# An attention and two dense layers on one core: the start addresses of the tiles in SBUF are shifted

## The chip, the cores and the metric

The kernel runs on one core of a Trainium2 chip. The metric is the time of one execution on the device in microseconds (us). The kernel before was timed three times: 1668.88, 1672.46 and 1673.58 us, median 1672.46. Everything read from a trace below belongs to one further, profiled execution.

## The reference

Three stages follow each other. All inputs and results are float32.

```python
# attention: q, k, v are (8, 8, 576, 64); p is (8, 8, 32, 64)
p_packed = softmax(p @ k.T / 8) @ v
x = softmax(q @ p_packed.T / 8) @ p_packed          # -> (4608, 512)
# layer 1: w_in (512, 2048), w_out (2048, 512); a has 4 numbers, b has 2
h = x @ w_in
g = (a0 + a1*h + a2*h**2 + a3*h**3) / (1 + |b0|*|h| + |b1|*h**2 + 1e-6)
x = g @ w_out
# layer 2: w2_in (512, 2048), w2_out (2048, 512), alpha (2048,)
h = x @ w2_in
out = (max(h, 0) + alpha * min(h, 0)) @ w2_out
```

The weights come as 64-bit numbers, are rebuilt as float32 on the chip, and each float32 operand of a large matmul is split into a high and a low part of type fp32r. A product is then three matmuls (high by high, high by low, low by high).

## The kernel before, in words

**Stages.** The attention stage runs from 0 to about 221 us. It works in 16 steps (8 batches, two groups of four heads), with plain float32 matmuls of 256 or 288 columns (L237, L250, L265, L289), and writes its result to DRAM. In the same time the weights of layer 1 are loaded and split, and `emit_Wb` (L334) multiplies `w_in` by the packed values of the attention (`pph`, which lies in `spw` on the right for even pairs of batches, the first pair's until 111 us among them, and in `gp` on the left for odd ones), so that layer 1 works on 256 instead of 512 inputs. Layer 1 follows, from about 221 to 870 us, and layer 2, from 870 us to the end.

**Layer 1.** The tokens come in 9 chunks of 512, the 2048 inner columns in 8 parts, which makes 72 steps `g`. A step has `emit_L1` (L470: first product into `h`; a chunk crosses a batch border, so its matmuls are 64 to 512 columns wide), `emit_E1` and `emit_E2` (the rational function on DVE, ACT and POOL) and, three steps later, `emit_L2` (L541: 24 matmuls of 512 columns). Beside this DVE, ACT and POOL rebuild the weights of layer 2 (`w2_step`; L568 to L598). Two PSUM buffers hold `h`, so that L470 of a step waits until E2 of two steps earlier is done.

**Layer 2.** 9 chunks by 16 inner parts make 144 steps. Each has 12 matmuls of `emit_L3` (L660), the activation (`emit_prelu`), and 12 matmuls of `emit_L4` (L741). All are 512 columns wide, and each has its own weight load of 128 columns.

**Which operand streams.** A matmul loads one operand of 128 columns as weights, and the other, the moving operand, streams through the array. The moving operands are `a2t` (L470), `gt` (L541), `yt` (L660) and the `w2_out` tiles `wo` (L741); the weights are `wb`, `wo`, `wb` and `vt`.

**Order.** The program is in written order on each engine (`manual_schedule`, L46): the loops at L383 to L391 for the attention, the letters of `ORDER` and `DRAIN` for the order inside, the loops at L684 and L754 for the layers.

**Layout of SBUF.** [...] Pools on the left side are stacked upwards from the bottom, pools on the right side downwards from the top, and a tile takes a multiple of 32 bytes. At the bottom lie the scratch of 1024 bytes (L801), four framework constants (128 bytes), then `const` with `ident` (512), `coef` (32), `alpha_sb` (64), `babs` (32) and `qc` (32): 1824 bytes, which is 3 x 512 + 288. Every later tile that the layers use on the left (`wp`, `gp`, then `spa` or `spb`) is a multiple of 512 bytes long, so all of them start at 288 bytes past a multiple of 512. On the right 32 bytes are in use at the very top, and the tiles of `spx` (`a2t`) and of `spy0`, `spy1` (`yt`) start at 480 bytes past a multiple of 512. The slices that a matmul reads are multiples of 512 bytes from there, with the exception of `a2t`, where a piece may begin at an odd multiple of 256 bytes. From the sizes follows also that the third `gt` buffer covers bytes 196384 to 204575 of a partition, and `yt` of the odd chunks (`spy1`) bytes 196576 to 212959.

The pool `sp0` (L163) holds the tiles of the attention alone; its space is used again by `spa` (L457) and `spb`. `ident` is the unit matrix by which TensorE transposes (L250, L251, L276).

Of the kernel before, what the change touches and what calls it, by code (L numbers as in the profile page):

```python
# [10 lines left out]
F32 = mybir.dt.float32  # L11
# [15 lines left out]
def attention_then_two_moes(ctx, tc, qT, kT, v, pT, w_in, w_out, ab, w2_in, w2_out, alpha, out):  # L27
    nc = tc.nc
# [18 lines left out]
    const = ctx.enter_context(tc.tile_pool(name="const", bufs=1))  # L47
# [1 line left out]
    gp = ctx.enter_context(tc.tile_pool(name="gp", bufs=1))  # L49
    dr = ctx.enter_context(tc.tile_pool(name="dr", bufs=1, space=DRAM))  # L50

    ident = const.tile([128, 128], F32, name="ident")
    make_identity(nc, ident)
    coef = const.tile([128, 6], F32, name="coef")
    nc.sync.dma_start(out=coef, in_=ab)
    alpha_sb = const.tile([128, NF], F32, name="alpha_sb")
# [2 lines left out]
    act(babs, coef[:, 4:6], AF.Abs)  # L59
    qc = const.tile([128, 1], F32, name="qc")  # L60
    pool.memset(qc, 1.0 + 1e-6)
    a0, a1c, a2c, a3 = (coef[:, i:i + 1] for i in range(4))
    b0, b1 = babs[:, 0:1], babs[:, 1:2]

# [88 lines left out]
    def open_pool(name, **kw):  # L153
        opened[name] = ExitStack()
        return opened[name].enter_context(tc.tile_pool(name=name, reuse_waits="tile", **kw))
# [7 lines left out]
    sp0 = open_pool("sp0", bufs=2, side="left")  # L163
    ps0 = open_pool("ps0", bufs=1, space=PSUM, side="left")

    mask = sp0.tile([128, 128], F32, tag="mask", name="mask", bufs=1)
    pool.memset(mask, 0.0)
    for h in range(4):
# [640 lines left out]
```

## Time and profile before

| what | value |
|---|---|
| median of three runs | 1672.46 us |
| profiled execution | 1673.79 us |
| span of its trace | 1672.0 us |
| PE busy | 1595.5 us (95%) |
| PEld (weight loads) busy | 1294.1 us (77%) |
| DVE busy | 1089.8 us (65%) |
| ACT busy | 778.4 us (47%) |
| POOL busy | 627.4 us (38%) |
| granted clock of TensorE over the span | 0.984 |

Engines are PE (TensorE's matmuls), PEld (its weight loads), DVE, ACT, POOL, and SP, which issues DMAs. A busy PE is not a PE at its peak: a matmul counts as busy from its start to its modelled end, and consecutive ones overlap. The rate is read from start to start.

### The profile page before, as it was taken

How to read it: one execution, taken by the hardware profiler on the slowest of the kernel's cores; microseconds unless marked ns; L12 is line 12 of the kernel's file. 1: busy time of each engine (PE TensorE's matmuls, PEld its weight loads, DVE VectorE, ACT ScalarE, POOL GpSimd, SP SyncE). 2: the span in 40 equal slices, each digit the busy share in tenths (PEclk: the TensorE clock that was granted, in tenths of full speed). 3: DMA queues.
4: the chain of work that ended last, by engine and by line, in shares of the span. 5: the costliest groups of instructions: out<-in, count | busy, mean ns of one | idle time of the engine just before them, and what ended most of it. 6: DMA issues, size and time to landing. Idle time of an engine off the chain costs nothing.

```text
span 1672.0 us, 19305 instructions
## 1 busy us (share of the span) xinstructions
PE 1595.5 (95%) x7424; PEld 1294.1 (77%) x7424; DVE 1089.8 (65%) x1323; ACT 778.4 (47%) x979; POOL 627.4 (38%) x369
## 2 busy tenths in 40 slices
PE   4878879999999999999999999999999999999999
PEld 2444557888888888888888888888888888888887
DVE  6988877999999999999954344344343434343343
ACT  3444578888889888887851111111111111111111
POOL 3443458777887888866650000000001010000000
PEclk9898999999999999999999999999999999999999
DMA  8889962324224242333561010101010101010000
GB/s 304 266 298 323 293 214 85 130 76 138 102 102 138 89 139 102 108 128 121 186 243 47 0 51 0 51 1 51 0 44 7 44 7 44 7 44 7 9 17 25
DMA packets 86683, 169.03 MB, mean 101 GB/s; under 512 B 8000, under 2 KB 45888, under 8 KB 86592
## 3 DMA queue, kind: packets, MB, share of 16 engines
q1 hardware_dynamic: 81984, 151.03, 26.6%
q10 hardware_dynamic: 4608, 16.78, 2.9%
q8 instruction: 58, 0.95, 0.2%
q14 instruction: 33, 0.27, 0.0%
HBM read 110.64 MB, written 57.15 MB: 100 GB/s over the span
## 4 chain that ended last, share of the span: by engine, by line
PE 76%; DVE 9%; DMA 6%; ACT 5%; issue 2%; POOL 2%; SPq 0%; ACTq 0%; POOLq 0%; DVEq 0%
PE u L660 24%; PE acc L741 24%; PE acc L541 16%; PE h L470 10%; DMA s<-in_w_out 3%; DMA wb_d<-wbs 1%; PE pw L334 1%; DVE s L585 1%; DVE h L526 1%; ACT h L521 1%; DVE s L584 1%; PE pp L265 1%; DMA kt<-in_kT 1%; DMA qt<-in_qT 0%; DVE mag L126 0%
## 5 line engine op out<-in xcount | busy, mean ns | idle before, releaser
L660 PE MATMUL u<-yt,wb 128*128 128x512 f32 x1728 | 425.9, 394 | 0.0
L741 PE MATMUL acc<-wo,vt 128*128 128x512 f32 x1728 | 417.4, 390 | 0.0
L541 PE MATMUL acc<-gt,wo 128*128 128x512 f32 x1728 | 406.1, 391 | 0.9 <-ACT yo L486 0.8
L670 ACT ACTIVATE vt<-m 128x512 fp32r<-128x512 f32 x144 | 91.0, 632 | 634.7 <-DVE m L668 634.7
L660 PEld LDWEIGHTS u<-yt,wb 128*128 128x128 f32 x1728 | 323.3, 187 | 77.8
L741 PEld LDWEIGHTS acc<-wo,vt 128*128 128x128 f32 x1728 | 324.2, 188 | 72.3
L541 PEld LDWEIGHTS acc<-gt,wo 128*128 128x128 f32 x1728 | 321.6, 188 | 66.5 <-ACT yo L486 1.6
L667 DVE TENSOR_SCALAR m<-u,alpha_sb 128x512 f32<-128x512 f32 x144 | 108.0, 750 | 317.1 <-PE u L660 317.1
L650 POOL TENSOR_TENSOR yt<-s,yt 128x512 fp32r<-128x512 f32 x36 | 46.7, 1300 | 646.5 <-ACT yt L649 646.5
L470 PE MATMUL h<-a2t,wb 128*128 128x128 f32 (+7 forms) x1536 | 247.2, 317 | 11.9 <-DVE v__1950 L527 6.8
L470 PEld LDWEIGHTS h<-a2t,wb 128*128 128x128 f32 x1536 | 228.3, 191 | 31.3 <-ACT q__1997 L507 7.2
L671 DVE TENSOR_TENSOR vt<-m,vt 128x512 fp32r<-128x512 f32 x144 | 99.6, 692 | 112.6 <-ACT vt L670 112.6
L668 DVE SCALAR_TENSOR_TENSOR m<-u,m 128x512 f32<-128x512 f32 x144 | 99.6, 692 | 5.0
L427 POOL TENSOR_TENSOR wb<-s,wb 128x512 fp32r<-128x512 f32 x64 | 83.9, 1314 | 37.6 <-ACT wb L426 37.5
L334 PE MATMUL pw<-wb,pph 128*128 128x512 f32 x192 | 63.1, 457 | 18.6 <-ACT wbs L346 17.0
L334 PEld LDWEIGHTS pw<-wb,pph 128*128 128x128 f32 x192 | 36.3, 209 | 44.7 <-ACT wbs L346 27.1
L575 DVE TENSOR_SCALAR s<-s 128x512 f32<-128x512 f32 x32 | 50.5, 1579 | 0.0
L598 POOL TENSOR_TENSOR s<-s 128x512 fp32r<-128x512 f32 x32 | 43.0, 1344 | 18.0 <-ACT s L597 18.0
L237 PE MATMUL ps<-kt,pt 128*64 128x288 f32 x128 | 27.0, 558 | 23.7 <-ACT a L243 8.0
L265 PE MATMUL pp<-vt,a1T 128*128 128x256 f32 (+1 forms) x160 | 45.3, 425 | 3.0 <-DMA vt<-in_v 2.3
L346 ACT ACTIVATE wbs<-pw 128x512 f32<-128x512 f32 x56 | 33.0, 591 | 27.6 <-PE pw L334 13.6
L265 PEld LDWEIGHTS pp<-vt,a1T 128*128 128x128 f32 (+1 forms) x160 | 32.0, 211 | 17.3 <-issue 9.3
(1006 smaller groups left out, 2000.3 us busy)
## 6 DMA issues: line engine op xcount, KB each, us to landing
wb_d<-wbs SPq DMA_DIRECT2D x64, 256.0 KB, 4.8
s<-wb_d SPq DMA_DIRECT2D x64, 256.0 KB, 3.7
w_d<-s SPq DMA_DIRECT2D x32, 512.0 KB, 2.6
kt<-in_kT SPq DMA_DIRECT2D x16, 576.0 KB, 6.2
qt<-in_qT SPq DMA_DIRECT2D x16, 576.0 KB, 6.2
y_d<-yo SPq DMA_DIRECT2D x18, 512.0 KB, 3.6
s<-y_d SPq DMA_DIRECT2D x36, 256.0 KB, 3.5
out<-o SPq DMA_DIRECT2D x36, 256.0 KB, 2.1
```

The costliest lines, as they stand in the source:

```text
L265: mm(pp, at[0:kc, c, :], v_[0:kc, c, :], start=c == 0, stop=c == 4)
L334: mm(pw, pph[bp][:, x, j].rearrange("p a b -> p (a b)"), w[:, y, :], start=k == 0, stop=k == 2)
L427: pool.tensor_tensor(t[:, 1], st, t[:, 0], op=ALU.subtract)
L470: mm(h[:, ft, o:o + m], w[x][:, k, 128 * ft:128 * ft + 128], a2_t[c][:, y, k, o:o + m], start=n == 0, stop=n == 5)
L541: mm(acc[d // 2][:, d % 2, :], w[:, x, 128 * d:128 * d + 128], t[:, y, ft, :], start=f == 0 and (x, y, ft) == (0, 0, 0), stop=f == NP - 1 ...
L575: dve.tensor_scalar(w, w, LOW, HIGH, op0=ALU.max, op1=ALU.min)
L660: mm(us[g], w2i[f][:, 1 - x, k, :], yt[c][:, y, k, :], start=n == 0, stop=n == 11)
L667: dve.tensor_scalar(m, u, 0.0, alpha_sb[:, f:f + 1], op0=ALU.min, op1=ALU.mult)
L668: dve.scalar_tensor_tensor(m, in0=u, scalar=0.0, in1=m, op0=ALU.max, op1=ALU.add)
L670: act(t[:, 0], m, AF.Copy)
L671: dve.tensor_tensor(t[:, 1], m, t[:, 0], op=ALU.subtract)
L741: mm(acc2[s], t[:, x, 128 * s:128 * s + 128], w2o[f][:, 1 - y, :], start=f == 0 and n == 0, stop=f == NF - 1 and n == 2)
```

## The change

`ident` moves from the pool `const` to the pool `sp0`, and is built there just before `mask`. Two tiles that nothing reads or writes are added: `fill_left` of 224 bytes at the end of `const`, and `fill_right` of 480 bytes at the top of the right side. With that `const` ends at 1536 bytes (3 x 512), the right side begins at 228864 bytes (447 x 512), and every tile of the two layers, on both sides, starts at a multiple of 512. No instruction is added or removed.

```diff
-    ident = const.tile([128, 128], F32, name="ident")
-    make_identity(nc, ident)
     coef = const.tile([128, 6], F32, name="coef")
...
     qc = const.tile([128, 1], F32, name="qc")
     pool.memset(qc, 1.0 + 1e-6)
+
+    const.tile([128, 56], F32, name="fill_left")
+    top = ctx.enter_context(tc.tile_pool(name="top", bufs=1, side="right"))
+    top.tile([128, 120], F32, name="fill_right")
...
     ps0 = open_pool("ps0", bufs=1, space=PSUM, side="left")
 
+    ident = sp0.tile([128, 128], F32, tag="ident", name="ident", bufs=1)
+    make_identity(nc, ident)
     mask = sp0.tile([128, 128], F32, tag="mask", name="mask", bufs=1)
```

## Rows read from the trace of the kernel before

**Rows 1.** The page's parts 1 and 4: busy us, shares; the chain by engine.
```profile
PE 1595.5 (95%) x7424; PEld 1294.1 (77%) x7424; DVE 1089.8 (65%) x1323; ACT 778.4 (47%) x979; POOL 627.4 (38%) x369
...
PE 76%; DVE 9%; DMA 6%; ACT 5%; issue 2%; POOL 2%; SPq 0%; ACTq 0%; POOLq 0%; DVEq 0%
```

**Rows 2.** Busy time of each engine in four stretches and the end of layer 1; clock and DMA last.
```profile
core 0: us, PE busy (x) PEld busy (x) DVE busy (x) ACT busy (x) POOL busy (x), PEclk, DMA share, GB/s
300.00:453.00 153.00, 153.00 (x818) 135.45 (x818) 144.07 (x123) 133.25 (x141) 119.87 (x62) 1.00 0.32 111
453.00:626.00 173.00, 170.62 (x966) 150.25 (x965) 166.54 (x143) 155.60 (x166) 142.58 (x73) 1.00 0.34 118
626.00:870.00 244.00, 244.00 (x1220) 210.26 (x1220) 216.46 (x186) 200.37 (x206) 172.72 (x86) 1.00 0.40 141
...
848.00:870.00 22.00, 22.00 (x98) 18.20 (x97) 9.39 (x8) 10.67 (x12) 12.27 (x7) 1.00 0.66 247
...
870.00:1672.00 802.00, 798.10 (x3458) 647.59 (x3456) 319.33 (x451) 118.39 (x194) 41.57 (x32) 1.00 0.08 27
```

**Rows 3.** The chain by line in the same four stretches, in that order.
```profile
by line: PE acc L541 60.8%; PE h L470 39.4%
...
by line: issue 13.2%; DVE s L585 6.4%; DVE s L584 5.8%; ACT h L521 5.2%; DVE h L526 4.7%; ACT wb L426 3.1%; DMA s<-wb_d 2.6%; PE h L470 2.3%; ACT s L597 2.2%; ACT a2t L414 1.8%; POOL q__3862 L509 1.4%; POOL q__4488 L509 1.4%; POOL q__3945 L
...
by line: PE acc L541 65.4%; PE h L470 34.7%
...
by line: PE u L660 50.2%; PE acc L741 49.2%; DVE o L747 0.1%; PE acc L541 0.1%; issue 0.0%
```

**Rows 4.** Timeline of PE, one step of layer 2: start, duration to the modelled end.
```profile
1199.96 2.96 PE L660 MATMUL u<-yt,wb 128*128 128x512 f32 x12
1202.76 2.90 PE L741 MATMUL acc<-wo,vt 128*128 128x512 f32 x12
1205.50 0.39 PE L660 MATMUL u<-yt,wb 128*128 128x512 f32 x1
```

**Rows 5.** The chain in layer 1: start, us until the next piece.
```profile
439.05 5.44 PE acc L541 x24
...
812.56 2.80 PE h L470 x12
...
848.62 21.78 PE acc L541 x96
```

**Rows 6.** Matmuls of one line: duration ns minimum/median/maximum, first and last start.
```profile
L660 PE MATMUL u<-yt,wb x1728: 394/394/395, 870.2 to 1656.8; 128*128 128x512 f32 x192
...
L741 PE MATMUL acc<-wo,vt x1728: 388/389/398, 881.4 to 1667.7; 128*128 128x512 f32 x192
...
L541 PE MATMUL acc<-gt,wo x1728: 387/389/501, 245.9 to 870.0; 128*128 128x512 f32 x192
...
L334 PE MATMUL pw<-wb,pph x46: 387/398/796, 66.1 to 111.0; 128*128 128x512 f32 x46
...
L265 PE MATMUL pp<-vt,a1T x6: 377/378/379, 169.4 to 170.5; 128*128 128x256 f32 x6
```

**Rows 7.** Timeline of PE: those six plain float32 matmuls.
```profile
169.45 1.46 PE L265 MATMUL pp<-vt,a1T 128*128 128x256 f32 x6
```

**Rows 8.** Groups of L470 by width: busy us, mean ns, idle before.
```profile
L470 PE MATMUL h<-a2t,wb 128*128 128x512 f32 x192 | 51.6, 421 | 10.2 <-DVE v__1950 L527 6.8 <-DVE v__2067 L527 2.5 <-DVE v__2250 L527 0.9
...
L470 PE MATMUL h<-a2t,wb 128*128 128x256 f32 x192 | 24.0, 281 | 0.9 <-DVE v__4653 L527 0.9
```

**Rows 9.** Timeline of the first microseconds: POOL, and PE's first use of `ident`.
```profile
0.72 0.20 POOL masks.py:197 MEMSET ident<- 128x128 f32 x1 [0.29 <-POOLq L800]
...
1.53 0.70 POOL L170 MEMSET mask<- 32x64 f32 x4
...
4.05 0.85 POOL L179 TENSOR_SCALAR pt<-pt 128x256 f32<-128x256 f32 x1 [1.81 <-DMA pt<-in_pT]
...
18.81 1.11 PE L250 MATMUL pst<-ident,a 128*128 128x128 f32 x4
```

**Rows 10.** Last use of `ident`, and first instruction on `spa`'s space: first and last start.
```profile
L276 PE MATMUL pp<-ident,ppn x16: 270/328/477, 31.7 to 208.1; 128*128 128x128 f32 x16
...
L506 ACT ACTIVATE r__1948<-h x1: 1025/1025/1025, 224.1 to 224.1; 128x1024 f32<-128x1024 f32 x1
```

## The prediction

> **What bounds the kernel now.** I read the page's busy shares first, then its chain, then both by stretch, and last the timeline of single matmuls. PE is busy for 95% of the span and holds 76% of the chain [rows 1]. Layer 2, from 870 us on, is PE alone: L660 and L741 make 99% of its chain, DVE works 319 of 802 us, and the granted clock is 1.00, that is 2.4 GHz [rows 2, 3]. Nothing there waits. So the only thing that can change is how long one matmul occupies the array.
>
> That time is the finding. In a step of layer 2 twelve matmuls of L660 take from 1199.96 to 1202.76, 233.3 ns each, and twelve of L741 until 1205.50, 228.3 ns each [rows 4]. In layer 1, 24 of L541 take 5.44 us, 226.7 ns each, and twelve of L470 at 512 columns take 2.80 us, again 233.3 ns [rows 5]. Widths, clock and weight loads are alike; the rates are not. The two slow lines stream their moving operand from the right side of SBUF (`yt`, `a2t`), the two faster ones from the left (`wo`, `gt`). The modelled durations say it too, by line and with hardly any spread: 394 ns for all 1728 of L660, a median of 389 for L541 and L741 [rows 6].
>
> How far is this from the best that the trace shows? The plain float32 matmuls of the attention, L265, have a duration of 378 ns, and six of them end 1.46 us after the first start, so they start (1460 - 378) / 5 = 216 ns apart [rows 6, 7]. At 2.4 GHz 216 ns are 518 clock periods for 256 columns: two periods a column, and 6 over. A matmul that takes one period a column and pays the same 6 needs 512 + 6, which is 216 ns again. Against that the left side pays 11 ns too much on each matmul and the right side 17.5. The duration is the interval plus 162 ns in all three cases (378 - 216, 389 - 227, 394 - 233), so the excess lies in streaming and not in starting or ending.
>
> Layer 1 has two limits. From 300 to 453 and from 626 to 870 us its chain is L541 and L470 alone; from 453 to 626 it changes among DVE, ACT and POOL [rows 3]. DVE is busy for 144 of 153, 167 of 173 and 216 of 244 us [rows 2].
>
> **Why the address may be the cause.** What separates right from left is either the height in the partition or the start address within some block. Height I can exclude by the layout: the third `gt` buffer and `yt` of the odd chunks share bytes 196576 to 204575, yet no L660 is fast [rows 6], and the last 96 of L541, which pass through all three buffers, take 21.78 us, 226.9 ns each [rows 5]. What remains is the start, 288 against 480 bytes past a multiple of 512. Both are 32 past a multiple of 64, so a block of 64 bytes can't tell them apart; blocks of 128, 256 or 512 can. A second reading is the distance between the weights' start and the moving operand's (0 for L541 and L741, 192 for L660 and L470). L334 speaks against it: for the first pair of batches its moving operand is on the left and its weights on the right, and its fastest last 387 ns, as L541's do [rows 6]; their median is 398, with other work around them, so this is weak.
>
> [...]
>
> **The change part by part.**
> *Layer 2.* If the excess goes at an address of 0, twelve matmuls take 12 x 215.8 = 2.59 us. L660 falls from 2.80 to 2.59. L741 falls from 2.74 to 2.61: 0.02 us of its 2.74 are above 12 x 226.7 and stay. The step falls from 5.54 to 5.20 us; 144 steps save 49 us. The trace has no matmul with a start at 0, so the ends are: nothing saved, and on the other side a loss, priced below. I take the 216 ns of L265, because that row shows the array taking 512 periods with no excess where the operand is asked for at half the rate. DVE's 319 of 802 us leave no new bound behind it [rows 2].
> *Layer 1.* L541: 72 x 24 x 10.9 ns = 19 us less PE time. L470: widths of 256 to 512, 192 matmuls each [rows 8], have 192 x 1920 columns, at 17.5 ns for 512 that is 12.6 us; narrower ones I count at nothing, since their weight loads (PEld) set their pace. Together 31 us less, but DVE has only 9 + 6 + 28 us of idle time in the three stretches, and 13 of these lie after 848 us, where its work is over [rows 2]. So 30 is a ceiling, and with DVE's work coming in uneven steps I take less than half: 12 us, between 0 and 30. What is late next is DVE, through L527 and the two `h` buffers. The last 96 matmuls of L541 [rows 5] have no such limit: 96 x 11 ns, 1 us.
> *Attention.* Its float32 matmuls pay no excess now. The transfers change their SBUF address; 6% of the chain, 100 us, is DMA [rows 1]. No row prices this; at the 3% by which PE's two sides differ it would be 3 us either way, and I take 0.
> *`ident` built later.* Two POOL instructions of 0.5 us change places with one of 0.1. POOL is done with `mask` at 2.2 us and waits for a DMA until 4.05, and PE first needs `ident` at 18.81 [rows 9]. Cost 0; without that cover 0.5 us, once. SP's and ACT's queues are not passed.
> *`ident` in `sp0`.* Its bytes pass to `r_` of `spa`, so L506 gets a further tile to wait for. The last transpose with `ident` starts at 208.1, L506 at 224.1 [rows 10]: 16 us of cover. Were it gone, L506 and all of step 0 behind it would be late by what is missing.
>
> Sum: 49 + 12 + 1 = 62 us off the profiled execution's 1673.8, that is 1612. This execution is 1.3 us above the median of the runs, so I say 1611.
>
> **Rivals.**
> 1. *Both sides level out at the left side's rate.* Distance to the weights, or a block in which 0 is no better than 32, would do it. L660 falls to 12 x 226.7 = 2.72 us, 11.5 us over 144 steps, L470 adds some 2. Time 1659. For it: 226.7 is the best fp32r rate of 512 columns in long rows. Against it: L334, above. Values between 216 and 227 belong here too, down to some 1638.
> 2. *Slower: streams on one residue collide.* PE reads weights and moving operand at once; with all starts at 0 both reads begin in the same place of a block, and each matmul pays the right side's price or more. At 233.3 ns for all, L741 loses 0.06 x 144 = 9 us and L541 0.16 x 72 = 11.5: time 1693. At 240, one step of 6.7 ns further, another 40: 1733. It decides from where the mean of L660 and L741 passes today's 230.8. For it: nothing says that the cost falls monotonically from 224 over 32 to 0. Against it: with both on the same residue now, L541 and L741 are the faster ones.
> 3. *The start doesn't matter at all*, and right and left differ for a cause that I don't see: nothing is saved, 1672. For it: no row has two starts on one side. Against it: the shared bytes, above, which leave little else. [...]
>
> **How the numbers follow.** Forecast (216 to 220 ns) 0.48; rival 1 with what lies between 0.20; rival 2 0.21; rival 3 0.11. Faster by over 0.3% (5 us, about what a measurement here can tell from no change) holds the first two, 0.68; within it 0.11; slower 0.21. The forecast's own range is 1594 (30 us from layer 1) to 1637 (220 ns, which gives back 4.2 ns x 3456, and 0 from layer 1). For eight in ten it has to reach over rivals 1 and 3 and the mild half of rival 2: 1597 to 1693.
>
> **What would show it.** In the timeline a step of layer 2 falls from 5.54 to about 5.2 us, and the durations of L660, L741 and L541 all become about 378 ns. In layer 1 the chain goes over from L541 and L470 to DVE, L527 and the weights' L584, L585, and DVE's idle time shrinks. Attention still ends near 221 us. Durations of 389 for all would show rival 1, above 394 rival 2, unchanged ones rival 3. Durations that fall while the time does not would mean that the address acts and something else binds.

## The result, and the profile after

The changed kernel takes 1657.31 us (median of 4 runs, 1655.85 to 1658.22). Its ratio to the kernel before (by then four runs, median 1673.02) is 0.9908, with a 95% interval of 0.9888 to 0.9929: 0.9% faster, some 15 us. Forecast were 1611 us, so the direction was right and the size was not. The time lies close to that of rival 1, 1659.

The page of the kernel after, parts 1 and 4, beside [rows 1]; four lines were added above the layers, so L660 is now L664, L741 is L745, L541 is L545 and L470 is L474.

```profile
PE 1579.8 (95%) x7424; PEld 1294.3 (78%) x7424; DVE 1089.0 (66%) x1323; ACT 777.4 (47%) x979; POOL 626.3 (38%) x369
...
PE 74%; DVE 9%; ACT 6%; DMA 6%; issue 3%; POOL 2%; SPq 0%; ACTq 0%; POOLq 0%; DVEq 0%
```

PE's busy time falls by 15.7 us, about as much as the span (1672.0 to 1656.4); the other engines keep theirs. The timeline of PE in layer 2, beside [rows 4]: start, duration to the modelled end.

```profile
1198.18 2.88 PE L664 MATMUL u<-yt,wb 128*128 128x512 f32 x12
1200.90 2.88 PE L745 MATMUL acc<-wo,vt 128*128 128x512 f32 x12
1203.62 2.88 PE L664 MATMUL u<-yt,wb 128*128 128x512 f32 x12
```

Both halves of a step take 2.72 us, 226.7 ns a matmul. L660 had 2.80 and L741 had 2.74. All matmuls of a line, minimum/median/maximum in ns, beside [rows 6]:

```profile
L664 PE MATMUL u<-yt,wb x1728: 388/389/390, 869.1 to 1641.3; 128*128 128x512 f32 x192
...
L745 PE MATMUL acc<-wo,vt x1728: 388/389/390, 879.9 to 1652.2; 128*128 128x512 f32 x192
...
L545 PE MATMUL acc<-gt,wo x1728: 387/389/501, 244.5 to 868.8; 128*128 128x512 f32 x192
```

L660 came down from 394 to 389, the left side's figure; nothing reached 378. Layer 2, from the first L660 to the last L741, went from 797.5 us (870.2 to 1667.7) to 783.1 (869.1 to 1652.2): 14.4 us less, which is 0.08 x 144 = 11.5 for L660 and 0.02 x 144 = 2.9 for L741. From the first to the last L541 layer 1 took 624.1 us before [rows 6] and takes 624.3 now: no gain. What is left, some 1.5 us, lies ahead of layer 1, whose first L470 started at 221.0 and now at 219.4 us. I give it no cause: in the profiles of the six variants below this start lies anywhere from 213.6 to 223.8.

Busy time by stretch, beside [rows 2] (us, then each engine's busy time; clock and DMA last):

```profile
300.00:453.00 153.00, 153.00 (x815) 135.18 (x815) 143.53 (x123) 133.03 (x141) 119.21 (x61) 1.00 0.32 110
453.00:626.00 173.00, 171.30 (x966) 150.74 (x965) 166.53 (x143) 155.62 (x166) 142.60 (x74) 1.00 0.33 117
626.00:870.00 244.00, 243.81 (x1219) 210.60 (x1219) 216.34 (x186) 199.46 (x205) 171.85 (x85) 1.00 0.40 143
870.00:1656.00 786.00, 782.58 (x3453) 647.90 (x3451) 318.58 (x451) 118.52 (x194) 41.23 (x32) 1.00 0.08 27
```

DVE's share in layer 1 is what it was; the expected move of the chain to DVE did not come, since PE did not become faster there.

### The profile page after: what moved, and what is told of

It reads as the page before. It is cut to its first block, busy times and chain, and to the rows that moved or that the text cites. A ratio compares the mean times of both kernels' runs of the same rounds, so it can differ in the third digit from the quotient of the medians.

```text
span 1656.4 us, 19305 instructions
## 1 busy us (share of the span) xinstructions
PE 1579.8 (95%) x7424; PEld 1294.3 (78%) x7424; DVE 1089.0 (66%) x1323; ACT 777.4 (47%) x979; POOL 626.3 (38%) x369
## 4 chain that ended last, share of the span: by engine, by line
PE 74%; DVE 9%; ACT 6%; DMA 6%; issue 3%; POOL 2%; SPq 0%; ACTq 0%; POOLq 0%; DVEq 0%
PE acc L745 24%; PE u L664 24%; PE acc L545 15%; PE h L474 9%; DMA s<-in_w_out 4%; PE pp L269 1%; PE pw L338 1%; DMA wb_d<-wbs 1%; DVE h L530 1%; DVE s L588 1%; DVE s L589 1%; ACT h L525 1%; DMA kt<-in_kT 1%; DMA pt<-in_pT 0%; ACT wb L430 0%
## 5 line engine op out<-in xcount | busy, mean ns | idle before, releaser
L664 PE MATMUL u<-yt,wb 128*128 128x512 f32 x1728 | 414.6, 389 | 0.0
L745 PE MATMUL acc<-wo,vt 128*128 128x512 f32 x1728 | 414.6, 389 | 0.0
L545 PE MATMUL acc<-gt,wo 128*128 128x512 f32 x1728 | 406.2, 391 | 0.7 <-ACT yo L490 0.6
L745 PEld LDWEIGHTS acc<-wo,vt 128*128 128x128 f32 x1728 | 324.5, 188 | 67.2
L664 PEld LDWEIGHTS u<-yt,wb 128*128 128x128 f32 x1728 | 324.4, 188 | 67.2
L545 PEld LDWEIGHTS acc<-gt,wo 128*128 128x128 f32 x1728 | 321.7, 188 | 66.3 <-ACT yo L490 1.5
L474 PE MATMUL h<-a2t,wb 128*128 128x128 f32 (+7 forms) x1536 | 247.2, 317 | 12.0 <-DVE v__1955 L531 6.9
L474 PEld LDWEIGHTS h<-a2t,wb 128*128 128x128 f32 x1536 | 229.1, 191 | 30.8 <-ACT q__2002 L511 7.3
L588 DVE SCALAR_TENSOR_TENSOR s<-s,s 128x512 int32<-128x512 int32 x32 | 44.8, 1401 | 0.0
```

Of the source, the lines that this page charges most:

```text
L474: mm(h[:, ft, o:o + m], w[x][:, k, 128 * ft:128 * ft + 128], a2_t[c][:, y, k, o:o + m], start=n == 0, stop=n == 5)
L545: mm(acc[d // 2][:, d % 2, :], w[:, x, 128 * d:128 * d + 128], t[:, y, ft, :], start=f == 0 and (x, y, ft) == (0, 0, 0), stop=f == NP - 1 ...
L588: dve.scalar_tensor_tensor(wi, in0=words[:, :, 0], scalar=29, in1=wi, op0=ALU.logical_shift_right, op1=ALU.bitwise_or)
L664: mm(us[g], w2i[f][:, 1 - x, k, :], yt[c][:, y, k, :], start=n == 0, stop=n == 11)
L745: mm(acc2[s], t[:, x, 128 * s:128 * s + 128], w2o[f][:, 1 - y, :], start=f == 0 and n == 0, stop=f == NF - 1 and n == 2)
```

## The experiments

Two theories stood first. **D**: what counts is the distance between the start of the moving operand and that of the weights (rival 1's first reading). In what follows *distance* means that difference in bytes, modulo 256 once that period has been shown. **A**: the start of the moving operand counts, whatever the weights' start.

**Moved and half changes of the kernel.** Each is timed against the kernel before.

Both sides at 480 past a multiple of 512, by one line in the kernel before:

```diff
     pool.memset(qc, 1.0 + 1e-6)
+
+    const.tile([128, 48], F32, name="fill_left")
```

> The kernel before with one edit: a fill of 192 bytes on the left, so that both sides start at 480 past a multiple of 512, where the slow side was. Theory D: distance 0 for all, L660-to-L741 step 5.44 us, durations 389 ns for all, time as after the change, 1657. Theory A: all at the right side's 233.3 ns, durations 394, step 5.60 us, time about 1693.

Both sides at 288, by a fill at the top alone:

```diff
     pool.memset(qc, 1.0 + 1e-6)
+
+    top = ctx.enter_context(tc.tile_pool(name="top", bufs=1, side="right"))
+    top.tile([128, 48], F32, name="fill_right")
```

> The kernel before with one edit: a fill of 192 bytes at the top, so that both sides start at 288, with nothing moved on the left. Theory D and theory A both: 226.7 ns for all, 1657. If instead multiples of 512 matter in some other way (transfers, other engines), it stays above 1657 by that part.

`ident` moved, and both fills left out of the change:

```diff
-    const.tile([128, 56], F32, name="fill_left")
-    top = ctx.enter_context(tc.tile_pool(name="top", bufs=1, side="right"))
-    top.tile([128, 120], F32, name="fill_right")
```

> Only ident is moved to sp0, both fills are left out: left side 288 (two whole blocks of 256 lower than before), right side 480, as before. Theories D and A: no change, 1672. If the moved ident or the new neighbours of sp0 bring part of the gain, it shows here alone.

The change without its fill at the top:

```diff
-    top = ctx.enter_context(tc.tile_pool(name="top", bufs=1, side="right"))
-    top.tile([128, 120], F32, name="fill_right")
```

> Half of the change: ident moved and the left fill, no fill at the top. Left at 0, right at 480. Theory D: distance 480, which is 224 within 256: L660 back at 233.4, layer 2 about 797, time 1672, no gain although all left tiles lie at multiples of 512. Theory A or any gain from aligned starts as such: L541 and L741, both on the left, below 226.7.

The change without its fill on the left:

```diff
-    const.tile([128, 56], F32, name="fill_left")
```

> The other half: ident moved and the top fill, no fill on the left. Left at 288, right at 0: yt and a2t at multiples of 512. Theory D: distance -288, again 224 within 256: 233.4, layer 2 about 797, time 1672. Theory A: L660 as in the changed kernel, 226.7, time 1657.

| kernel | left, right | median us | ratio to before (95%) | layer 2, us |
|---|---|---|---|---|
| the change | 0, 0 | 1657.31 | 0.9908 (0.9888 to 0.9929) | 783.1 |
| both at 480 | 480, 480 | 1661.47 | 0.9928 (0.9908 to 0.9948) | 783.1 |
| both at 288 | 288, 288 | 1657.39 | 0.9912 (0.9889 to 0.9934) | 783.1 |
| `ident` only | 288, 480 | 1673.75 | 1.0001 (0.9985 to 1.0017) | 797.5 |
| left fill only | 0, 480 | 1675.63 | 1.0014 (1.0000 to 1.0028) | 798.4 |
| right fill only | 288, 0 | 1674.87 | 1.0019 (1.0006 to 1.0033) | 798.4 |

Theory A falls: with both sides at 480, where the slow stream was, all matmuls are fast, and `yt` at a multiple of 512 is slow when the weights are not. Each half of the change alone brings nothing. The gain is whole with no tile at a multiple of 512. With both at 480 the median lies 4 us higher; the two intervals overlap, its layer 2 is the same, and in its profile layer 1 starts at 223.8 instead of 219.4 us. The timeline of PE with both at 480 and, below, with the left fill only:

```profile
1201.08 2.88 PE L662 MATMUL u<-yt,wb 128*128 128x512 f32 x12
1203.80 2.88 PE L743 MATMUL acc<-wo,vt 128*128 128x512 f32 x12
1206.52 2.88 PE L662 MATMUL u<-yt,wb 128*128 128x512 f32 x12
```

```profile
1200.68 2.96 PE L662 MATMUL u<-yt,wb 128*128 128x512 f32 x12
1203.49 2.91 PE L743 MATMUL acc<-wo,vt 128*128 128x512 f32 x12
1206.23 2.96 PE L662 MATMUL u<-yt,wb 128*128 128x512 f32 x12
```

**Matmuls alone, starts swept.** One tile of weights, one of moving data, sections of 48 matmuls:

```python
mm(p[0:k, 0:n], wt[:, wo:wo + k], mv[:, mo:mo + n], ...)   # wo, mo: start + multiples of 512 and 2048 bytes
```

> Only matmuls: 36 sections of 48 fp32r matmuls, 128 weight columns by 512 moving columns unless said, the rest of the computation is left out. Weights slices start at W and moving slices at M bytes past a multiple of 512; the letter is the multiple of 32 (a is 0, g is 192). Theory D (what counts is the distance M - W): dist_a 226.7 ns per matmul, dist_g 233.3, all both_ (M = W) 226.7, the wei_ sections (M = 0, W moved) differ among themselves as the dist_ ones do. Theory A (what counts is M alone): all wei_ like dist_a, both_ like the dist_ of the same letter, so both_p 233.3 and both_j 226.7. If the excess over 216 ns comes from the weight loads that run beside, half_ and quar_ (64 and 32 weight columns) have less of it, about half and a quarter of 11 ns; if it belongs to the moving stream alone, they stay at 226.7 and 233.3.

The start of a section minus that of the one before, over 48, is the time of a matmul. The timeline of PE, some of the sections:

```profile
25.67 11.04 PE L54 MATMUL dist_a<-mv,wt 128*128 128x512 f32 x48
36.55 11.37 PE L54 MATMUL dist_b<-mv,wt 128*128 128x512 f32 x48
47.75 11.16 PE L54 MATMUL dist_c<-mv,wt 128*128 128x512 f32 x48
58.75 11.37 PE L54 MATMUL dist_d<-mv,wt 128*128 128x512 f32 x48
...
114.78 11.05 PE L54 MATMUL dist_i<-mv,wt 128*128 128x512 f32 x48
...
258.46 11.06 PE L54 MATMUL both_p<-mv,wt 128*128 128x512 f32 x48
269.36 11.36 PE L54 MATMUL wei_c<-mv,wt 128*128 128x512 f32 x48
...
291.72 11.16 PE L54 MATMUL wei_g<-mv,wt 128*128 128x512 f32 x48
302.71 11.07 PE L54 MATMUL wei_i<-mv,wt 128*128 128x512 f32 x48
```

Distance 0 costs (36.55 - 25.67) / 48 = 226.7 ns, 32 bytes 233.3, 64 bytes 229.2, 96 bytes 233.5; 128 to 224 give 233 to 234, and from 256 (`dist_i`) the series repeats. So the period is 256 bytes. With both starts moved together (`both_`) it is 227 throughout; moving the weights by 192 bytes (`wei_g`, distance -192, which is 64 within 256) gives the 229 of distance 64. Theory D holds for 512 columns. The weight loads' part was not as expected: with 64 weight columns distance 0 costs 230 and distance 192 costs 233, with 32 columns 232 both.

**What the last 11 ns are.** Distances in steps of 4 bytes, other widths, types and ways of reading, 48 matmuls each:

> Only matmuls again, 53 sections of 48, the rest of the computation left out; theory D now says that the interval follows the distance of moving operand and weights within 256 bytes, and asks where the last 11 ns at distance 0 come from. four_a to four_p: distances 0 to 60 bytes in steps of 4; down_b, c, e: -4, -8, -16. If the reads meet in lines of 16 bytes or more, four_b to four_d stay near 226.7; if word by word, they jump to 229 to 234 at once. Widths of 64 to 448 (roman figures) at distances 0, 64 and 192: if the excess belongs to each column, it grows with the width; if it is paid once per weight load, it is the same for all. Theory W (the last 11 ns are the weight load beside the stream): cols_ with 8 weight columns fall to about 216; rival S (they belong to a float32-wide stream, whatever runs beside): cols_viii stays above 226, half_ (bf16, half the bytes) goes to 216, and stay (one column read 512 times) tells whether the moving address matters. rows_ (64 and 32 rows): unchanged in both. full_ (plain float32, 256 columns): 216 at either distance.

> Only matmuls, 29 sections of 48 fp32r matmuls with 128 weight columns, the rest of the computation left out. It asks to whom the last 11 ns at distance 0 belong. Theory F (a fixed price for starting a stream of fp32r words at one a period): widths 256, 480, 496, 512 at distance 0 all lie 10.8 ns above columns / 2.4 GHz + 2.5, and reading the same slice again (same, sameboth) changes nothing. Rival C (a price per column or line that is read): times_ sections, which read 256, 128, 64, 32, 8, 4 or 2 different columns over and over to make 512, get cheaper with fewer different columns; step (every second column, twice the lines) gets dearer. A section at 216 ns with 512 different columns would be a way to a faster kernel.

Timeline of PE in the first of the two kernels, the sections that decide:

```profile
492.51 11.04 PE L67 MATMUL cols_viii<-mv,wt 128*8 128x512 f32 x48
503.39 10.53 PE L67 MATMUL half_a<-mh,wh 128*128 128x512 bf16 x48
513.77 10.52 PE L67 MATMUL half_g<-mh,wh 128*128 128x512 bf16 x48
524.13 20.88 PE L67 MATMUL full_a<-st 128*128 128x256 f32 x96
544.85 20.88 PE L67 MATMUL full_g<-st 128*128 128x256 f32 x96
565.38 10.71 PE L67 MATMUL stay<-mv,wt 128*128 128x512 f32 x48
```

And in the second:

```profile
157.47 11.04 PE L64 MATMUL times_h<-mv,wt 128*128 128x512 f32 x48
168.35 11.52 PE L64 MATMUL times_p<-mv,wt 128*128 128x512 f32 x48
179.71 10.55 PE L64 MATMUL times_z<-mv,wt 128*128 128x512 f32 x48
190.11 10.52 PE L64 MATMUL times_y<-mv,wt 128*128 128x512 f32 x48
200.47 10.52 PE L64 MATMUL times_x<-mv,wt 128*128 128x512 f32 x48
210.83 21.96 PE L64 MATMUL step<-mv,wt 128*128 128x512 f32 x48
232.61 11.39 PE L64 MATMUL back<-mv,wt 128*128 128x512 f32 x48
```

With a weight load of only 8 columns beside it, an fp32r matmul at distance 0 still takes 226.7 ns; with 64 columns it takes 230. So the load beside the stream has some part, but not the one that theory W gave it: theory W falls. The bf16 matmul takes 216 at either distance, and so does plain float32 with 256 columns, `full_` (48 of these are recorded as 96 matmuls, 215.8 ns each) [here and in rows 7]. That much of rival S holds.

Reading one column 512 times (`stay`, after its first matmuls), or 2, 4 or 8 columns over and over (`times_x`, `_y`, `_z`), takes 216 to 217 ns too. But 256, 128 or 64 different columns cost the full 226.7, and 32 (`times_p`) cost 237. Every second column of a range twice as long (`step`) takes (232.61 - 210.83) / 48 = 454 ns, twice 227.

Neither explanation on record covers this. Reading the same slice again (`same`, `sameboth`) changes nothing, as theory F said. But its constant surcharge falls with `times_x` and with the widths: above columns / 2.4 + 2.5 ns (the 6 periods of the prediction, an estimate from L265), distance 0 costs 10.8 ns at 256, 320 and 384 columns, 13 to 14 at 448, 480 and 496, and 10.9 at 512. The 2.4 columns a ns show in the widths: alone at distance 0 and at a granted clock of 0.99 to 1.00, 256 columns take 120.2 ns, 384 take 173.3 and 512 take 226.7, which is 0.416 ns a column. Rival C, a price per column or line that is read, falls as well: half the memory, 256 columns, pays as much as 512, and fewer different columns are no cheaper down to 32 (16 were not tried). What the last 11 ns are stays open.

Steps of 4 bytes give from 229 to 240 ns, so the starts count to the single word; the four dearest distances, 4, 20, 36 and 52 (237 to 240), lie 16 bytes apart. No section with 512 different columns of fp32r came below 226.7.

**Distance 64 in the kernel**, with a top fill 64 bytes shorter:

```diff
-    top.tile([128, 120], F32, name="fill_right")
+    top.tile([128, 104], F32, name="fill_right")
```

> The changed kernel with the top fill 64 bytes shorter: left at 0, right at 64. Theory D with the interval measured alone at distance 64 (228.8 ns): L660 12 x 228.8 = 2.745 us, L741 2.72 to 2.74, a step 5.47 to 5.49 us, layer 2 from 786 to 789 us (783.1 at distance 0, 797.5 before), time about 1661. A rule that asks for a whole block of 128 bytes or more would put it back to 797 and 1672.

This missed: 1671.82 us, ratio 0.9993 (0.9975 to 1.0011), layer 2 796.4 us. The timeline of PE:

```profile
1196.68 2.93 PE L664 MATMUL u<-yt,wb 128*128 128x512 f32 x12
1199.44 2.93 PE L745 MATMUL acc<-wo,vt 128*128 128x512 f32 x12
1202.21 2.93 PE L664 MATMUL u<-yt,wb 128*128 128x512 f32 x12
```

L660 takes 2.76, and L741, at distance 0, takes 2.77 instead of 2.72 us. Start to start, the matmuls of L741 come after 234, 231, 233, 236, 224, 231, 236, 228, 232, 231, 227, 227 ns: ten of twelve pass before the pace is the settled one. In the kernel before it was five, 226, 236, 228, 233, 231. To see whether other engines have a part in it, twelve matmuls at one distance and twelve at 0 took turns alone:

> Only matmuls, the rest of the computation left out: sections of 192 matmuls of 512 columns, in which twelve at one distance (the letter times 32 bytes) and twelve at distance 0 take turns, as L660 and L741 do in layer 2. Theory T (a change of the distance costs some matmuls until the pace settles, with no other engine's part in it): 24 matmuls take 5.44 us for a, 5.54 for g (192, the kernel before) and 5.53 for c (64, where the kernel gained nothing), although c alone has 228.8 ns. If what kept distance 64 from gaining in the kernel was other work (DVE's reads of PSUM, the weights' places), c takes 12 x 228.8 + 12 x 226.7 = 5.47 us here.

```profile
57.38 43.68 PE L47 MATMUL turn_a<-mv,wt 128*128 128x512 f32 x192
...
145.38 44.43 PE L47 MATMUL turn_c<-mv,wt 128*128 128x512 f32 x192
...
322.77 44.48 PE L47 MATMUL turn_g<-mv,wt 128*128 128x512 f32 x192
```

Over the middle six turns 24 matmuls take 5.440 us at distance 0, 5.533 at 64 and 5.540 at 192 (5.527 to 5.573 at the five others), which are the steps of the changed kernel, of distance 64 and of the kernel before to 0.01 us. Theory T holds: the starts alone, with no other engine at work, give the three times of layer 2.

## Why the prediction was right or wrong

**Right.** Layer 2 is bound by the rate of single matmuls, and the starts of the tiles set that rate; `ident` costs nothing (1.0001). Excluding the height in the partition was right: in the sections of matmuls alone both operands lie low on the left side, and they show 226.7 and 233.3 ns all the same.

**The step that failed** is "If the excess goes at an address of 0, twelve matmuls take 12 x 215.8 = 2.59 us", with the choice of L265's 216 ns behind it. L265 walks over its memory at half the rate, as the text itself said (256 columns in 216 ns), and such a matmul takes the same 215.8 ns at both distances tried (`full_a` 0, `full_g` 192). An fp32r stream of 512 columns still takes 11 ns more, 226.7, at the best of the distances tried: that it pays only the 6 periods of L265 was an estimate, and no section with 512 different fp32r columns shows it. The 2.4 GHz under it stand in no row; as 2.4 columns a ns the sections of other widths show them (0.416 ns a column, above). Of the right side's 17.5 ns only the 6.7 above 226.7 could be had. The term of 49 us for layer 2 measured 14.4. The left side's 226.7 was no sign of a start 32 bytes off; it was already the best.

**The reading that was set aside was the right one.** Rival 1 named the distance to the weights and got 0.20, because L334's fastest matmuls last 387 ns with weights on the other side. That row can't tell the two readings apart. By the layout the first pair's weights start at 480 and its moving operand at 288, a distance of -192, which is 64 within 256, and at 64 single intervals of 226 ns occur as they do at 0: from start to start L334's shortest take 225 and 226 ns for the first pair and 224 and 226 for the second, at distance 0. The durations agree: the second pair of batches, with both operands on the left, has the same (387 at least, median 399), and after the change, with equal starts, the first pair has 387 and 397.

Rival 1's time came out partly by luck. Its 11.5 us for L660 were measured to 0.1 us; its 2 us for L470 did not come, and L741's 2.9 us and the 1.5 us ahead of layer 1 stood in no rival's sum.

**L741's 0.02 us** were taken to stay. They were the cost of the first five matmuls after each change to distance 0, and went: 2.9 us.

**Layer 1** was given 12 us and got none. L541 was at the best distance before, so its 19 us of PE time were not there to gain. Narrow L470 was rightly counted at nothing: from start to start 64, 128 and 192 columns take 110 or 111 ns before and 111 or 112 after, and in the stretch of 64 and 128 columns alone, below, PEld is busy for 40.00 of 40.00 us. In the chain after, a step of 384 and 128 columns and, further down, one of 512 columns read (start, us until the next piece):

```profile
641.81 3.42 PE h L474 x24
645.23 5.54 PE acc L545 x24
...
828.42 2.72 PE h L474 x12
831.14 5.44 PE acc L545 x24
```

and the first of the two in the kernel before:

```profile
642.66 3.40 PE h L470 x24
646.06 5.52 PE acc L541 x24
```

At 512 columns L470 fell from 2.80 [rows 5] to 2.72; in the split step L470 and L541 became 0.02 us longer each. By chunk, over the steps in which no other engine held PE up, the medians of L470 and L541 together change by -0.10 us at 512 columns and by -0.02 to +0.07 us, on average +0.03, at the seven splits. Sixteen steps of the first kind and 56 of the others make -1.6 and +1.5 us: an estimate from the two traces, and it leaves nothing, as measured. Alone, 320 columns take 146.6 ns at distances 0, 64 and 192. For 256 columns distance 0 takes 120 in three runs, and distance 192 takes 117.7 in one and 113.7 in two. So at other widths an equal start brings nothing or costs a little, and at 256 columns the distance by itself does not fix the pace. Whether DVE would have been the next limit was not put to the test.

**Rival 2** has no case in it: equal starts are the best of the 25 distances within 256 bytes that were tried at 512 columns. **Rival 3** fell with the durations of L660, 394 ns before and 389 after.

## What to carry to other kernels

Where equal fp32r matmuls of 512 columns run at two rates, compare the start of the moving operand with that of the weights modulo 256 bytes, and make the two equal for all matmuls that follow each other (alone 226.7 ns at equal starts, 229 to 240 at the 24 other distances). Where both then lie is free: 0, 288 and 480 past a multiple of 512 gave the same layer 2, and bringing one side alone to a multiple of 512 brought nothing. At other widths, measure first; at 256 columns the equal start was slower (120 ns) than distances 64 and 192 (118, and 114 to 118). A floor must come from a row that asks for the same: the 216 ns of float32 with 256 columns and of bf16 with 512 were no floor for fp32r, which took 226.7 at best with 512 different columns. Where two distances take turns, count the change as well: in turns of twelve the matmuls at distance 0 took five to settle after distance 192 and ten after distance 64, and of the 8 to 11 us that distance 64 was expected to save in layer 2, 1.1 were left.

## What was not expected of the hardware

With matmuls of 64 columns and 128 weight columns the granted clock fell. Two stretches of the kernel that swept the widths, the first of the two above (us, busy times, clock behind the engines):

```profile
195.00:225.00 30.00, 30.00 (x132) 24.44 (x131) 1.50 (x3) 0.00 (x0) 0.00 (x0) 1.00 0.06 14
...
260.00:300.00 40.00, 40.00 (x189) 40.00 (x189) 1.06 (x4) 0.00 (x0) 0.00 (x0) 0.50 0.06 14
```

Up to 238.69 us PE ran 512 columns, with a clock of 1.00 from 195 to 225 us, then 64 columns at 116 ns each on average; from 260 to 300 us, with 64 and 128 columns, the clock is 0.50, and a matmul takes 213 ns, although PE counts as busy throughout. In the sections of 192 columns that followed the clock rose again (0.99 from 300 to 380 us). The same kernel was expected to show no effect of fewer rows. With 64 rows the matmuls take 230 and 235 ns on average at distances 0 and 192, 227 and 233 with 128 rows; with 32 rows of 512 columns the clock fell as well (0.61 from 420 to 470 us), and a matmul took 429 ns on average at distance 192.
